# Two half-experts move from plain products to block products, and pure weight blocks are fetched raw, split and written back

## The chip, the cores and the metric

The kernel runs on one core of a Trainium2 chip. The metric is device time in microseconds (us), lower is better; a kernel's time is the median of several runs. Beside the runs there is one profiled execution, whose trace is read here.

## The reference, cut to what matters

```
x   = local_attention(q, k, v)                      # 2304 tokens x 512
x   = elu(x @ w_in) @ w_out                         # first MLP, 2048 hidden
P   = sinkhorn(exp(x @ w_gate - max), 8 rounds)     # 2304 x 8
out = 0
for e in range(8):                                  # w1[e]: 512x1024, w2[e]: 1024x512
    h   = maximum(x @ w1[e], 0)
    out += P[:, e:e+1] * (h @ w2[e])
```

All of it is float32. Only the last loop, the eight experts, is touched by the change.

## The kernel before, in words

TensorE multiplies in the type fp32r. To keep float32 accuracy every operand is split into a high part (a copy rounded to fp32r, made by ACT) and a low part (operand minus high part, made by DVE or POOL), and every product is three matmuls: high·high, high·low, low·high.

The tokens are in three groups of 768 (g = 0, 1, 2), in halves of TH = 384. An expert is two half-experts (512 of its 1024 hidden columns each; index 2·e + pp). A half-expert can be done for a group in two ways.

*Plain*: ordinary products (`e_in` for the first layer, `e_out` for the second). The first PU half-experts are done so, for group 0 alone.

*Block products*: the operands are cut 2x2, and seven products of sums of blocks (`l1` first layer, `l2` second layer) stand for eight. One half-expert of one group is a **period** of seven steps. A step has two `l1` products (6 matmuls of 384 columns each) and one `l2` product; `l2` runs LAG = 8 steps behind `l1`. Of the seven weight blocks of such a set three are **pure**, that is, plain blocks of w1 or w2 (slots 0 to 2), and four are sums (slots 3 to 6). Periods run over the rest of group 0, then all half-experts of group 1, then of group 2.

Split weight blocks lie in DRAM (`wd1`, `wd2`: slot, high and low part) before a period reads them. They are made in three places: `q_tasks(.., "pre")` in the middle of the first MLP (N1 half-matrices), `p_tasks` from the last quarter of the first MLP through the plain stage (N3 half-matrices first, then for each plain unit its four and some others in between, paced by the table `due`), and `late_tasks` in the first block-product periods (`tail`). In `p_tasks` POOL makes the sums, ACT and DVE split them, and SP issues the loads and stores; a half-matrix whose split form a plain unit needs keeps it in SBUF too.

In the block-product stage the order on each engine's queue is the order in which the program emits. `w1_load` and `w2_load` (SP) fetch blocks NW1 = 12 and NW2 = 7 products ahead. After a product ACT copies its PSUM tile out (`a`, `u`, `v`, `r`), DVE adds (`c`, `s`), ACT makes high parts (`h`), DVE or POOL low parts (`hid_low`). PSUM holds two tiles `la`, two `lb`, and one each of `oa` and `ob`. A chain accumulates its `la` tile over several products, so the next product into it waits for the copy; the products 7 and 4 of a chain share one `lb` tile, so product 4 waits for DVE to have read product 7 (the add into `c22`), and the product 7 of the next chain needs the tile that the add into `c21` frees. In group 0 DVE also adds each `l2` product into `acc`.

## Time and profile before

| | |
|---|---|
| median of 3 runs | 1964.22 us (1964.12 to 1965.58) |
| time of the profiled execution | 1965.19 us |
| its span, first to last instruction | 1963.4 us |
| TensorE busy in the span | 1948.9 us |
| granted TensorE clock, mean | 0.999 of full speed |
| plain stage in the trace | from about 499 to 809 us |
| block products of group 0 in the trace | from 809.27 us, seven periods |

The profiled execution is 0.97 us above the median of the runs, so a difference worked out in its trace is set against the median. Where the profile groups matmuls, their durations overlap; the distance from start to start is the cost of one.

### The profile page before, as it was taken

How to read it: one execution, taken by the hardware profiler on the slowest of the kernel's cores; microseconds unless marked ns; L12 is line 12 of the kernel's file. 1: busy time of each engine (PE TensorE's matmuls, PEld its weight loads, DVE VectorE, ACT ScalarE, POOL GpSimd, SP SyncE). 2: the span in 40 equal slices, each digit the busy share in tenths (PEclk: the TensorE clock that was granted, in tenths of full speed). 3: DMA queues.
4: the chain of work that ended last, by engine and by line, in shares of the span. 5: the costliest groups of instructions: out<-in, count | busy, mean ns of one | idle time of the engine just before them, and what ended most of it. 6: DMA issues, size and time to landing. Idle time of an engine off the chain costs nothing.

```text
span 1963.4 us, 33821 instructions
## 1 busy us (share of the span) xinstructions
PE 1948.9 (99%) x11898; PEld 1818.1 (93%) x11898; DVE 1509.2 (77%) x2567; ACT 860.4 (44%) x1821; POOL 732.0 (37%) x718
## 2 busy tenths in 40 slices
PE   8999999999999999999999999999999999999999
PEld 6888888898888888999999999999999999999998
DVE  6756676767797655687787888888887888888886
ACT  8885555555543433444343333333334333333332
POOL 4523232334355553443343333233253333232231
PEclk9999999999999999999999999999999999999999
DMA  9742354469799999699778777788888887777783
GB/s 205 191 93 56 107 173 151 153 219 323 274 377 378 378 361 340 235 360 340 242 249 310 259 260 263 240 275 259 293 263 253 256 271 263 261 261 260 235 280 118
DMA packets 311191, 495.17 MB, mean 252 GB/s; under 512 B 80352, under 2 KB 162416, under 8 KB 307312
## 3 DMA queue, kind: packets, MB, share of 16 engines
q1 hardware_dynamic: 309840, 492.73, 76.2%
q8 instruction: 95, 1.56, 0.3%
q14 instruction: 72, 0.59, 0.1%
q10 hardware_dynamic: 1184, 0.30, 0.1%
HBM read 361.78 MB, written 126.95 MB: 249 GB/s over the span
## 4 chain that ended last, share of the span: by engine, by line
PE 95%; ACT 3%; DVE 2%; DMA 0%; issue 0%; SPq 0%; DVEq 0%; ACTq 0%
PE la L1127 16%; PE lb L1127 12%; PE oa L1207 12%; PE ob L1207 11%; PE ob L1272 3%; PE oa L1272 3%; PE p L932 3%; PE p L933 3%; PE p L934 3%; PE ac L950 3%; PE ac L951 3%; PE p L213 3%; PE p L212 3%; PE ac L547 3%; PE ac L548 3%; PE ac L549 3%
## 5 line engine op out<-in xcount | busy, mean ns | idle before, releaser
L1109 POOL TENSOR_TENSOR h<-s,h 128x384 fp32r<-128x384 f32 x312 | 363.7, 1181 | 725.6 <-ACT h L1100 700.3
L1127 PE MATMUL la<-xf,w1f 128*128 128x384 f32 x1872 | 369.6, 335 | 1.4 <-ACT u L1147 1.3
L1127 PEld LDWEIGHTS la<-xf,w1f 128*128 128x128 f32 x1872 | 326.4, 188 | 2.6 <-ACT u L1147 2.1
L1127 PE MATMUL lb<-xf,w1f 128*128 128x384 f32 x1404 | 281.1, 334 | 0.0
L1100 ACT ACTIVATE h<-s 128x384 fp32r<-128x384 f32 x312 | 159.2, 522 | 246.8 <-DVE s L1151 239.8
L1207 PE MATMUL ob<-h,w2f 128*128 128x384 f32 x1344 | 252.3, 335 | 0.0
L1207 PE MATMUL oa<-h,w2f 128*128 128x384 f32 x1344 | 252.0, 335 | 0.2 <-DVE acc L1224 0.2
L1127 PEld LDWEIGHTS lb<-xf,w1f 128*128 128x128 f32 x1404 | 246.1, 188 | 0.0
L1207 PEld LDWEIGHTS oa<-h,w2f 128*128 128x128 f32 x1344 | 234.4, 188 | 0.5 <-DVE acc L1224 0.5
L1207 PEld LDWEIGHTS ob<-h,w2f 128*128 128x128 f32 x1344 | 234.4, 188 | 0.1
L1105 DVE SCALAR_TENSOR_TENSOR h<-c,h 128x384 fp32r<-128x384 f32 x234 | 193.0, 835 | 32.2 <-ACT h L1100 31.4
L1100 ACT ACTIVATE h<-c 128x384 fp32r<-128x384 f32 x234 | 122.8, 525 | 176.0 <-DVE c L1137 161.8
L739 POOL TENSOR_TENSOR sw<-rw 128x256 f32<-128x256 f32 x104 | 94.8, 912 | 183.8 <-DVE g L775 110.9
L1137 DVE TENSOR_TENSOR c<-c,pb 128x384 f32<-128x384 f32 x192 | 144.5, 752 | 6.6
L1224 DVE TENSOR_TENSOR acc<-ob,acc 128x768 f32<-128x768 f32 (+1 forms) x114 | 105.0, 924 | 37.4 <-PE ob L1207 37.4
L1224 DVE TENSOR_TENSOR acc<-oa,acc 128x768 f32<-128x768 f32 (+1 forms) x110 | 101.2, 923 | 37.3 <-PE oa L1207 37.3
L1151 DVE SCALAR_TENSOR_TENSOR s<-c,s 128x384 f32<-128x384 f32 x156 | 109.7, 703 | 13.4 <-DMA out_dram<-ost 2.4
L1147 ACT ACTIVATE v<-la 128x384 f32<-128x384 f32 x78 | 38.3, 491 | 162.0 <-PE la L1127 161.9
L254 ACT ACTIVATE hh<-p 128x512 fp32r<-128x512 f32 (+1 forms) x72 | 35.3, 490 | 161.9 <-PE p L934 161.7
L932 PE MATMUL p<-xh,f 128*128 128x256 f32 (+1 forms) x288 | 97.8, 339 | 0.0
L933 PE MATMUL p<-xl,f 128*128 128x256 f32 (+1 forms) x288 | 96.9, 336 | 0.0
L934 PE MATMUL p<-xh,f 128*128 128x256 f32 (+1 forms) x288 | 96.9, 336 | 0.0
(176 smaller groups left out, 3895.4 us busy)
## 6 DMA issues: line engine op xcount, KB each, us to landing
w1f<-wdi SPq DMA_DIRECT2D x546, 256.0 KB, 3.9
w2f<-wdo SPq DMA_DIRECT2D x273, 512.0 KB, 4.1
rw<-in_moe_w_dram SPq DMA_DIRECT2D x208, 128.0 KB, 4.8
wdi<-g SPq DMA_DIRECT2D x26, 1024.0 KB, 7.0
wdo<-g SPq DMA_DIRECT2D x26, 1024.0 KB, 7.4
wdi<-f SPq DMA_DIRECT2D x26, 768.0 KB, 5.1
wdo<-f SPq DMA_DIRECT2D x26, 768.0 KB, 5.3
raw<-in_moe_w_in_dram SPq DMA_DIRECT2D x16, 512.0 KB, 4.2
```

The source lines that it names most:

```text
L932: nc.tensor.matmul(p1[:, :n], w[:, s, 0, cs], xh, start=(c == 0), stop=False)
L933: nc.tensor.matmul(p1[:, :n], w[:, s, 0, cs], xl, start=False, stop=False)
L934: nc.tensor.matmul(p1[:, :n], w[:, s, 1, cs], xh, start=False, stop=(c == NCC - 1))
L1100: nc.scalar.activation(h[:, 0], src, AF.Relu if relu else AF.Copy)
L1105: nc.vector.scalar_tensor_tensor(h[:, 1], src, 0.0, r(h[:, 0]), op0=ALU.max, op1=ALU.subtract)
L1109: nc.gpsimd.tensor_tensor(out=h[:, 1], in0=src, in1=r(h[:, 0]), op=ALU.subtract)
L1127: nc.tensor.matmul(o, w[:, a, c, :], x[:, b, c, :], start=first and c == 0 and z == 0, stop=last and c == 1 and z == 2, skip_group_check=True,
L1137: nc.vector.tensor_tensor(out=t, in0=t, in1=pb[g, e][:, i], op=ALU.mult)
L1151: nc.vector.scalar_tensor_tensor(d[nm], d[a], 0.0, d[b], op0=ALU.max, op1=op)
L1207: nc.tensor.matmul(o[:, c], w[:, p, b, c * P:(c + 1) * P], hs[p][:, a, :], start=fresh and p == 0 and z == 0, stop=False, skip_group_check ...
L1224: nc.vector.tensor_tensor(out=a, in0=src, in1=a, op=ALU.add)
L1272: nc.tensor.matmul(o[:, c * HB2:(c + 1) * HB2], hs[p][:, a, c * P:(c + 1) * P], w[:, p, b, :], start=fresh and c != 1 and p == 0 and z == ...
```

## The change: what it does

- PU goes from 9 to 7: two half-experts of group 0 move from the plain stage to block products, which has 41 periods where it had 39. N1, N3 and the tail become 11, 10 and 5 half-matrices; the ten others are spread evenly over the plain units (`mids`), one or two for each, and `p_tasks` splits no pure blocks for half-matrices that no plain unit uses.
- Pure blocks are no longer stored by `p_tasks` or `q_tasks`; these store the sums alone.
- In the nine group-0 periods, and in the first seven periods of group 1, pure blocks are loaded raw from w1 or w2 (`raw_at`) into tiles `r1` (4 buffers) and `r2` (3), half the bytes of a split block. `w_part` makes the high part on ACT and the low part on POOL (w1), or on DVE in group 0 and POOL in group 1 (w2). `w_back` stores the split block to DRAM, where later groups read it. Such a period has six raw w1 blocks and three raw w2 blocks.
- To make room NW1 goes from 12 to 9 and NW2 from 7 to 6. `w_part` stands four `l1` products, or two steps, ahead of its use, in the emitted order.

```diff
-    PU, N1, N3 = 9, 9, 9
-    tail = [(E - 1) * 2 * NP + i for i in (5, 6, 7)]
+    PU, N1, N3, LATE = 7, 11, 10, 5
+    tail = list(range(E * 2 * NP - LATE, E * 2 * NP))
...
-        if u >= 2 and rest:
-            hs.insert(1, (rest.pop(0), u % 4))
+        for i, h in enumerate(mids[u]):
+            hs.insert(2 * i + 1, (h, None))
...
-            p_high(h, 0)
+            if h not in quiet:
+                p_high(h, 0)
...
-    NW1, NW2, LAG = 12, 7, 8
+    NW1, NW2, LAG = 9, 6, 8
...
+    def raw_at(k, s):
+        g, e, pp = periods[k]
+        return s < 3 and (g == 0 or (g == 1 and 2 * e + pp < PU))
+
+    def w_part(key):
+        if key not in apart:
+            return
+        a, hi, lo, t, to, g = apart.pop(key)
+        nc.scalar.activation(hi, a, AF.Copy)
+        sub = nc.gpsimd if key[0] == 1 else (nc.vector, nc.gpsimd)[g]
+        sub.tensor_tensor(out=lo, in0=a, in1=r(hi), op=ALU.subtract)
+        back[key] = (to, t)
+
+    def w_back(key):
+        if key in back:
+            to, t = back.pop(key)
+            nc.sync.dma_start(out=to, in_=t)
...
+        for n in range(4):
+            w_part((1, n))
+        w_back((1, 0))
...
                     w1_load(s * 2 + z + NW1)
+                    w_part((1, s * 2 + z + 4))
+                    w_back((1, s * 2 + z + 1))
...
+            ahead = 0 if s == 3 else s - LAG + 2
+            if s == 3 or ahead > 0:
+                w_part((2, ahead))
+            w_back((2, 0 if s == 4 else s - LAG + 1))
             while late:
                 late.pop(0)()
```

How this moves instructions shows at three places. The first is DVE's queue in the first block-product period, after its step 3. Names: `s` and `c` are the sums, `lb` the PSUM tile, `w2f` a split w2 block, `r_8338` a raw one. Before:

```order
L1151 SCALAR_TENSOR_TENSOR s_9002<-c_8938,r_9000 128x384 [waits DMAHW0_49,Activation_49]
L1151 SCALAR_TENSOR_TENSOR s_9004<-c_8974,r_9000 128x384
L1151 SCALAR_TENSOR_TENSOR s_9006<-c_8938,s_9004 128x384 [waits DVE_49]
L1141 TENSOR_TENSOR c_9024<-lb,u 128x384 [waits PE_49]
L1151 SCALAR_TENSOR_TENSOR s_9026<-c_9024,s_9006 128x384 [waits DVE_49]
L1141 TENSOR_TENSOR c_9037<-lb,a 128x384 [waits PE_49]
```

And of the change, at the same place:

```order
L1185 SCALAR_TENSOR_TENSOR s_8348<-c_8276,r_8346 128x384 [waits Activation_49]
L1185 SCALAR_TENSOR_TENSOR s_8350<-c_8314,r_8346 128x384
L1185 SCALAR_TENSOR_TENSOR s_8352<-c_8276,s_8350 128x384 [waits DVE_49]
L1064 TENSOR_TENSOR w2f<-r_8338,w2f 128x2x256 [waits DMAHW3_49,Activation_49]
L1175 TENSOR_TENSOR c_8375<-lb,u 128x384 [waits PE_49]
L1185 SCALAR_TENSOR_TENSOR s_8377<-c_8375,s_8352 128x384 [waits DVE_49]
L1175 TENSOR_TENSOR c_8388<-lb,a 128x384 [waits PE_49]
```

The low part of the first raw w2 block now stands ahead of the add `c<-lb,u`, and waits for ACT's high part, which stands behind the high part of `s_8352` on ACT's queue.

The second place is DVE's queue in the first period of group 1, steps 4 and 5, where group 0's last `l2` products are still added into `acc`. Before:

```order
L1288 SCALAR_TENSOR_TENSOR acc_103<-oa,Pr,acc_103 128x256 [waits PE_49]
L1288 SCALAR_TENSOR_TENSOR acc_103<-oa,Pr,acc_103 128x256 x2
L1167 TENSOR_TENSOR c_11725<-lb,v 128x384 [waits Activation_49]
L1137 TENSOR_TENSOR c_11725<-c_11725,pb 128x384 [waits DVE_49]
L1288 SCALAR_TENSOR_TENSOR acc_103<-ob,Pr,acc_103 128x256 [waits PE_49]
L1288 SCALAR_TENSOR_TENSOR acc_103<-ob,Pr,acc_103 128x256 x2
```

Of the change:

```order
L1322 SCALAR_TENSOR_TENSOR acc_103<-oa,Pr,acc_103 128x256 [waits PE_49]
L1322 SCALAR_TENSOR_TENSOR acc_103<-oa,Pr,acc_103 128x256 x2
L1064 TENSOR_TENSOR w2f<-r_11884,w2f 128x2x256 [waits DMAHW5_49,DMAHW4_49,Activation_49]
L1201 TENSOR_TENSOR c_12142<-lb,v 128x384 [waits Activation_49]
L1171 TENSOR_TENSOR c_12142<-c_12142,pb 128x384 [waits DVE_49]
L1322 SCALAR_TENSOR_TENSOR acc_103<-ob,Pr,acc_103 128x256 [waits PE_49]
L1322 SCALAR_TENSOR_TENSOR acc_103<-ob,Pr,acc_103 128x256 x2
L1064 TENSOR_TENSOR w2f<-r_11936,w2f 128x2x256 [waits DMAHW6_49,DMAHW0_49,Activation_49]
```

A low part of a w2 block follows the adds into `acc` in steps 4, 5 and 6 of a group-0 period.

The third place is SP's queue late in group 0. DMAHW0 to DMAHW7 are eight semaphores taken in turn: each transfer waits for the one eight before it. Before, in one step and a half:

```order
L1079 DMA w2f<-wdo_0_159 128x1024 [waits DMAHW7_49,PE_49]
L1068 DMA w1f<-wdi_2_141 128x512 [waits DMAHW0_49,PE_49]
L828 DMA wdo_1_162<-qf 128x2x512 [waits DMAHW1_49,DVE_49,Activation_49]
L1068 DMA w1f<-wdi_2_141 128x512 [waits DMAHW2_49,PE_49]
L1079 DMA w2f<-wdo_0_159 128x1024 [waits DMAHW3_49,PE_49]
L1068 DMA w1f<-wdi_3_142 128x512 [waits DMAHW4_49,PE_49]
```

Of the change (`r_` raw blocks, `wdi<-w1f` and `wdo<-w2f` the stores):

```order
L1107 DMA r_9927<-in_moe_w_dram 128x2x256 [waits DMAHW7_49]
L1086 DMA r_9944<-in_moe_w_dram 128x2x128 [waits DMAHW0_49,Pool_49]
L1070 DMA wdi_2_137<-w1f 128x512 [waits DMAHW1_49]
L1092 DMA w1f<-wdi_0_139 128x512 [waits DMAHW2_49,PE_49]
L1070 DMA wdi_3_138<-w1f 128x512 [waits DMAHW3_49,Pool_49]
L1113 DMA w2f<-wdo_1_158 128x1024 [waits DMAHW4_49]
L1092 DMA w1f<-wdi_0_139 128x512 [waits DMAHW5_49,PE_49]
L1092 DMA w1f<-wdi_0_139 128x512 [waits DMAHW6_49]
L1113 DMA w2f<-wdo_1_158 128x1024 [waits DMAHW7_49]
L1086 DMA r_10057<-in_moe_w_dram 128x2x128 [waits DMAHW0_49]
```

A period that had 21 transfers of 7.34 MB has 30 of 8.91 MB (14 w1 blocks, six of them raw with six stores; seven w2 blocks, three of them raw with three stores).

## Rows read from the trace of the kernel before

**Rows 1.** The page: busy time of the engines, share, instructions

```profile
PE 1948.9 (99%) x11898; PEld 1818.1 (93%) x11898; DVE 1509.2 (77%) x2567; ACT 860.4 (44%) x1821; POOL 732.0 (37%) x718
```

**Rows 2.** Waits of PE: who for whom, us in total, times, longest

```profile
PE la L1127 <- ACT u L1147: 1.3, 2, 1.0
```

**Rows 3.** PE's timeline, plain stage (start, us): a unit's start, four units later

```profile
641.35 0.39 PE L932 MATMUL p<-xh,f 128*128 128x512 f32 x1
...
773.51 0.39 PE L932 MATMUL p<-xh,f 128*128 128x512 f32 x1
```

**Rows 4.** PE's timeline, step 2 of periods: group 0 five apart; group 1 two apart

```profile
861.30 2.25 PE L1127 MATMUL la<-xf,w1f 128*128 128x384 f32 x12
...
1009.47 2.25 PE L1127 MATMUL la<-xf,w1f 128*128 128x384 f32 x12
...
1039.03 2.24 PE L1127 MATMUL la<-xf,w1f 128*128 128x384 f32 x12
...
1097.27 2.24 PE L1127 MATMUL la<-xf,w1f 128*128 128x384 f32 x12
```

**Rows 5.** Stretches: us, PE, PEld, DVE, ACT, POOL busy, clock, DMA share, GB/s

```profile
600.00:650.00 50.00, 50.00 (x257) 42.73 (x256) 34.52 (x44) 21.55 (x31) 29.37 (x35) 1.00 1.05 382
850.00:900.00 50.00, 50.00 (x357) 50.00 (x357) 40.98 (x76) 21.95 (x47) 22.27 (x22) 1.00 1.01 371
...
956.27:985.67 29.40, 29.40 (x211) 29.40 (x210) 22.13 (x44) 10.93 (x23) 11.03 (x9) 1.00 0.75 240
985.67:1015.07 29.40, 29.40 (x210) 29.40 (x209) 25.49 (x46) 14.73 (x28) 17.44 (x13) 1.00 0.81 273
```

**Rows 6.** Groups by form, 840 to 1000 us: busy, mean ns

```profile
L823 DVE TENSOR_TENSOR qf<-qw,qf 128x512 fp32r<-128x512 f32 x8 | 7.9, 992 | 0.0
...
L843 POOL TENSOR_TENSOR qw<-qw 128x256 f32<-128x256 f32 x12 | 9.5, 793 | 3.7 <-DVE qf L823 1.8 <-ACT a L1147 1.3
```

**Rows 7.** POOL's timeline at the start of the block products

```profile
803.14 3.64 POOL L1025 TENSOR_TENSOR xf<-xb,xf 128x768 fp32r<-128x768 f32 x2
818.50 5.17 POOL L1109 TENSOR_TENSOR h<-s,h 128x384 fp32r<-128x384 f32 x4 [11.72 <-ACT h L1100]
```

**Rows 8.** ACT's timeline there

```profile
818.96 0.94 ACT L1100 ACTIVATE h<-s 128x384 fp32r<-128x384 f32 x2 [0.54 <-DVE s L1151]
```

**Rows 9.** DVE's timeline there

```profile
813.56 0.56 DVE L1105 SCALAR_TENSOR_TENSOR h<-c,h 128x384 fp32r<-128x384 f32 x1 [1.35 <-ACT h L1100]
...
818.37 0.56 DVE L1151 SCALAR_TENSOR_TENSOR s<-c,s 128x384 f32<-128x384 f32 x1
818.84 0.55 DVE L1141 TENSOR_TENSOR c<-lb,u 128x384 f32<-128x384 f32 x1
...
820.61 2.19 DVE L1105 SCALAR_TENSOR_TENSOR h<-c,h 128x384 fp32r<-128x384 f32 x2
```

**Rows 10.** PE's timeline there

```profile
809.27 1.23 PE L1127 MATMUL la<-xf,w1f 128*128 128x384 f32 x6
...
819.70 1.21 PE L1127 MATMUL lb<-xf,w1f 128*128 128x384 f32 x6
...
822.86 1.81 PE L1272 MATMUL ob<-w2f,h 128*128 128x256 f32 x13 [0.19 <-DVE h L1105]
```

**Rows 11.** DVE's timeline, start of group 1

```profile
1012.34 0.55 DVE L1167 TENSOR_TENSOR c<-lb,v 128x384 f32<-128x384 f32 x1
...
1025.75 0.54 DVE L1167 TENSOR_TENSOR c<-lb,v 128x384 f32<-128x384 f32 x1
```

**Rows 12.** PE's timeline, the products that these adds let start

```profile
1014.75 1.20 PE L1127 MATMUL lb<-xf,w1f 128*128 128x384 f32 x6
...
1027.45 1.20 PE L1127 MATMUL lb<-xf,w1f 128*128 128x384 f32 x6
```

**Rows 13.** DMA issues, 820 to 1000 us: KB each, median us to landing

```profile
w1f<-wdi SPq DMA_DIRECT2D x89, 256.0 KB, 4.8
...
qw<-in_moe_w_dram SPq DMA_DIRECT2D x12, 128.0 KB, 5.8
```

More of the change, by code (lines that the diff above doesn't have):

```diff
@@ L701 @@
     rest = others[N1 + N3:]
+    mids = [[]]
+    for u in range(1, PU):
+        mids.append(rest[len(rest) * (u - 1) // (PU - 1):len(rest) * u // (PU - 1)])
     for u in range(PU):
         hs = [(4 * u + i, 4 + (4 * u + i - 4) % 8 if u else i) for i in range(4)]
-        if u >= 2 and rest:
-            hs.insert(1, (rest.pop(0), u % 4))
+        for i, h in enumerate(mids[u]):
+            hs.insert(2 * i + 1, (h, None))
         order += hs
@@ L760, in p_high @@
     def p_high(h, part):
-        n = 3 if part == 0 and h in quiet else 4
         b = slot_of[h]
@@ L768, in p_high @@
         src = (sws if part else rws)[h]
-        nc.scalar.activation(t[:, :n, 0, :], src[:, :n], AF.Copy)
+        nc.scalar.activation(t[:, :, 0, :], src, AF.Copy)
     def p_low(h, part):
-        n = 3 if part == 0 and h in quiet else 4
         t = (sums if part else forms)[h]
@@ L826, in low @@
             )
-            if a >= 4:
-                nc.sync.dma_start(out=to[:, a - 1:a + 1], in_=r(t))
-            else:
-                for i in range(n):
-                    s = [s for s in pos if pos[s] == a + i][0]
-                    nc.sync.dma_start(out=to[:, s], in_=r(t[:, i]))
+            nc.sync.dma_start(out=to[:, a - 1:a + 1], in_=r(t))
         def sums():
@@ L849, in q_tasks @@
             return load, [
[L850 to L852 removed]
+                sums, *[nothing] * 2, lambda: high(4, 2), lambda: (low(4, 2), high(6, 2)),
+                lambda: low(6, 2), *[nothing] * 2,
             ]
         return [
[L855 to L856 removed]
+            load, nothing, sums, nothing, lambda: high(4, 2),
             lambda: (low(4, 2), high(6, 2)), lambda: low(6, 2),
@@ L889, in highs @@
         def highs():
-            p_high(h, 0)
+            if h not in quiet:
+                p_high(h, 0)
             if n:
-                p_store(before, 1)
+                p_store(before)
         def last():
-            p_low(h, 0)
+            if h not in quiet:
+                p_low(h, 0)
             p_load(n + 3)
@@ L1067, in w1_load @@
         t = P2["w1p"].tile([P, 2, 2, P], R32, tag="w1", bufs=NW1, name="w1f")
-        nc.sync.dma_start(
-            out=r(t).rearrange("p z c f -> p z (c f)"), in_=wd1[e][2 * pp + p][:, SLA[pi]]
-        )
+        s = SLA[pi]
+        to = wd1[e][2 * pp + p][:, s]
+        if raw_at(k, s):
+            f, d = [fd for fd, v in PURE[0].items() if v == s][0]
+            f0 = f * (FF // 2) + (2 * pp + p) * P
+            a = P2["w1p"].tile([P, 2, P], F32, tag="r1", bufs=4, name="r1")
+            nc.sync.dma_start(
+                out=a,
+                in_=w1[e][d * 2 * P:(d + 1) * 2 * P, f0:f0 + P].rearrange("(c p) f -> p c f", p=P),
+            )
+            apart[1, n] = (a, t[:, 0], t[:, 1], r(t).rearrange("p z c f -> p z (c f)"), to, g)
+        else:
+            nc.sync.dma_start(out=r(t).rearrange("p z c f -> p z (c f)"), in_=to)
         w1t[n] = t
@@ L1078, in w2_load @@
         t = P2["w2p"].tile([P, 2, 2, HB2], R32, tag="w2", bufs=NW2, name="w2f")
-        nc.sync.dma_start(out=r(t), in_=wd2[e][pp][:, SLB[out_order[x]]])
+        s = SLB[out_order[x]]
+        to = wd2[e][pp][:, s]
+        if raw_at(k, s):
+            f, d = [fd for fd, v in PURE[1].items() if v == s][0]
+            f0 = f * (FF // 2) + 2 * pp * P
+            a = P2["w2p"].tile([P, 2, HB2], F32, tag="r2", bufs=3, name="r2")
+            nc.sync.dma_start(
+                out=a,
+                in_=w2[e][f0:f0 + 2 * P, d * HB2:(d + 1) * HB2].rearrange("(q p) d -> p q d", p=P),
+            )
+            apart[2, n] = (a, t[:, :, 0], t[:, :, 1], r(t), to, g)
+        else:
+            nc.sync.dma_start(out=r(t), in_=to)
         w2t[n] = t
```

28 lines of the change are left out of this document (10 added, 18 removed).

## The prediction

> **What bounds the kernel now.** I read the page first: PE is busy 1948.9 us of a span of 1963.4 [rows 1]. The rest is 14.5 us, about half of it in the first 50 us. The table of waits comes next: in all of the block products the largest wait of PE is 1.3 us in two pieces, for the copy `u` [rows 2]. The stretches then show PE at 50.00 of 50 us even where the DMA engines are saturated, at 382 GB/s in the plain stage and 371 in the first block products [rows 5]. So the kernel is bound by the matmuls that PE is given. DMA, POOL and ACT cost nothing as long as they are not late. The reader should take from this that a change can win only by giving PE fewer columns, and loses whatever new waits of PE it makes. DVE deserves a look too: 25.49 of 29.40 us in the period before group 1 [rows 5], with less slack than anything but PE.
>
> **What the change takes from PE.** A plain unit (one half-expert for group 0) starts at 641.35, the fifth at 773.51, so one lasts (773.51 - 641.35) / 4 = 33.04 us [rows 3]. A group-0 period lasts (1009.47 - 861.30) / 5 = 29.63 us [rows 4]. Two half-experts change from one to the other: 2 x (33.04 - 29.63) = 6.82 us less. Periods of groups 1 and 2, 29.12 us each [rows 4], keep their matmuls and their number. No PE wait elsewhere is there to be removed, so 6.8 us is the most that the change can bring.
>
> **What it adds, where hidden.** In a raw period ACT makes nine more copies. Two of 384 columns take 0.94 us [rows 8], so one of 256 or 512 is bounded by 0.4 and 0.7 us, together at most 4.5 us on top of 14.73 of 29.40 [rows 5]: hidden. POOL makes six subtractions of 256 columns at 0.79 us [rows 6], 4.8 us on top of 17.44 in its fullest period [rows 5]. In group 1 it makes three of 512 as well, 0.8 to 1.9 us each (the row of 256 and half of the 3.64 us that two of 768 take [rows 7]); I take 1.6, so 9.6 us on POOL in a raw period of 29.12 us. All this is hidden on average.
>
> At the stage's start POOL's last form ends at 803.14 + 3.64 = 806.78 [rows 7]; two low parts at 0.79 follow and the first is ready at 807.6, the second at 808.4, before PE's first product at 809.27 [rows 10]. If that 0.9 us of cover went, PE would wait by as much. In the plain stage 34 half-matrices are prepared in six units where 39 were in eight: POOL's work in a unit grows by about a sixth of 29.37 of 50 us [rows 5], DVE's and ACT's stays, the stores of pure blocks fall away. I cost it at nothing, at most 1 us if a form came late for its unit.
>
> **DVE, first place: the start of the block products.** In the first period the low part of the first raw w2 block stands ahead of the add `c<-lb,u`. In the trace the last `s` ends at 818.37 + 0.56 = 818.93, and that add stood at 818.84, with no gap [rows 9]. ACT's two high parts for `s` run from 818.96 [rows 8]; the new copy falls between them, at about 819.4, and ends about 820.0. The subtraction of 128x512 takes 0.99 us by the nearest row, for the same form [rows 6], so it ends near 821.0. The add then ends near 821.5. The product into the tile that it frees started at 819.70 [rows 10]: 1.85 us of wait. The chain behind (another `s`, the next `c`, two `h`) moves on by about 2.2 us, and the first `l2` product, which waited for it till 822.86 [rows 10], moves with it. I take 2.1 us; the bounds are 1.5 (a subtraction of 0.6 us, and POOL idle) and 2.8 (the raw block landing late: a load takes 4.8 to 5.8 us [rows 13], and is issued about 5 us after the stage starts).
>
> **DVE, second place: the start of group 1.** From about 997 to 1038 us DVE works almost without a gap: group 1's forms and scalings beside group 0's adds. Three low parts of w2 blocks come into this stretch, 3 x 0.99, and POOL's extra work slows DVE somewhat (below). The add `c<-lb,v` at 1012.34 ended 1.86 us ahead of the product that needs it, the one at 1025.75 only 1.16 us [rows 11, 12]. By then DVE would be about 2.3 and 2.4 us later (two low parts, 0.7 us of contention; after a gap, another low part): waits of 0.4 and 0.8 us, so 1.2 us. Bounds: 0, if gaps absorb it, and 2.5, if nothing does. In the other group-0 periods the same adds have 1.3 to 2 us to spare and DVE has gaps of some 4 to 7 us (22.13 of 29.40 busy [rows 5]); I take nothing.
>
> **DMA.** A raw period moves 8.91 MB where it moved 7.34: 8.91 / 29.63 us = 301 GB/s, under the 371 and 382 that the trace shows [rows 5]. In the first periods the tail's five half-matrices and the filling of w2 come on top. From the queue's order the periods' loads and stores sum to 7.9, 12.6, 11.5 and 10.5 MB, so 42.5 MB in four periods, 358 GB/s; the two worst need 425 and 389. At 371 GB/s (11.0 MB a period) the queue falls behind by 1.6 + 0.5 MB, some 6 us. A raw w1 block is issued five products, some 10.5 us, before ACT reaches its copy, and lands in about 5.8 us [rows 13]; the queue usually runs some products ahead of that, but the late stores make it wait for DVE. If 6 us of lag met 4.7 us of margin, ACT would hold up PE's copies by 1.3 us, of which a step covers most. I take 0.9 us, between 0 and 4.
>
> The sum: -6.82 + 2.1 + 1.2 + 0.9 = -2.6 us. The profiled execution, 1965.19 us, would become 1962.6. It stood 0.97 us above the median, and against that median of 1964.22 the forecast is **1961.6 us**, 0.13% less. Differences within 0.2%, 3.9 us, I count as no change; about that much can be told from none here.
>
> **A rule weighed against the rows.** DVE's low part `h<-c,h` takes 0.56 us alone at 813.56, and 2.19 us for two at 820.61, while POOL is busy from 818.50 to 823.67 [rows 7, 9]: an operation on two SBUF tiles is slowed, at most twofold. Work of POOL costs DVE about 0.2 us for each us here if their operations meet a third of the time, so 4.8 us of new POOL work costs some 1 us in a group-0 period, as taken above. The Trainium skill, "SBUF — State Buffer", section "SBUF: two separate sides", has it harder: VectorE with two SBUF inputs and GpSimd hold a shared port pair in turn, for the whole instruction, and the loser is blocked. Each 0.79 us subtraction could then stop DVE for its length. The trace agrees in kind (twofold at worst); in how often they meet it decides, and the full blocking is the third rival.
>
> **The rivals.**
>
> *Faster: the waits are hidden.* The new adds meet gaps; only part of the first place is left. With waits of 1.5 to 2.9 us the time is 1964.22 - 6.82 + 1.5 to 2.9, about 1959.2; with none it is 1957.4. For it: six periods in the trace go by with no wait at all and DVE at 75% to 87%. Against: the first place has its order written down, and no gap ahead of `c<-lb,u` [rows 9]. Chance 0.33.
>
> *Slower: the DMA queue cannot keep up.* Sixteen periods run raw. If blocks in pieces of 512 bytes and stores among loads lower the rate, raw blocks come after ACT has reached their copies, the copies `u` and `v` queue behind, and PE waits in every period. At 290 GB/s a period would take 8.91 / 0.290 = 30.7 us: 9 x 1.1 + 7 x 1.6 = 21 us, less some 9 us of lead (nine products are some 19 us; after landing split blocks keep 13 of them, raw ones 5), so +12, and with the other terms (-6.8 + 3.3) +8.6, 1972.8. At 300 it would decide near +3. For it: 358 GB/s are wanted over four periods. Against: the plain stage ran at 382 with raw loads and stores mixed [rows 5]. Chance 0.12.
>
> *No change, by another way: POOL blocks DVE.* If each new POOL subtraction stopped DVE for its whole length, a usual group-0 period had 22.13 + 3.0 + 4.8 = 29.9 of 29.63 us and the one before group 1 25.49 + 7.8 = 33.3: waits of about 8 x 0.3 + 3.7 = 6.1 us beside the first place's 2.1, so 1964.22 - 6.82 + 8.2 = 1965.6. Against: POOL's and DVE's operations meet only in part, since most adds read PSUM. Chance 0.10.
>
> My forecast itself has 0.45. So faster by over 0.2% 0.33, within 0.2% 0.55, slower 0.12. For the range: below 1957.4 nothing is left; the faster cases begin there, 1957.8 leaves out very little, and 1966.5 takes in the blocked DVE and a mild DMA lag. About 0.15 lies outside. The likeliest case's own range, from its bounds (1.5 to 2.8, 0 to 2.5, 0 to 4, cut at the bound for faster), is 1960.3 to 1964.5.
>
> **What would show it.** Right: two plain units fewer at 33.0 us, and two periods more at 29.6; a wait of PE of about 2 us for DVE's `c` or `h` within 15 us of the first block product; DVE above 95% in the period before group 1 with waits under 1 us each; landing of raw blocks below 8 us. Wrong: PE waiting for ACT's `u` and `v`, with ACT waiting for DMA, in many periods (the queue), or steady small waits for `c` in each raw period (the ports), or a start of group 1 as free of waits as before (the waits are hidden).

## The result, and the profile after

The changed kernel takes 1981.91 us (median of 4 runs, 1980.77 to 1983.18), the kernel before 1964.9 beside it: a ratio of 1.0086, 95% interval 1.0069 to 1.0104. The forecast of 1961.6 and its range up to 1966.5 were wrong; the change is slower by 17 us. The profiled execution has a span of 1981.4 us, 18.0 more than before.

The first line, of the page of the changed kernel, is to be read beside [rows 1]: PE still is nearly always busy. The view behind it cuts the trace at the starts of units and periods (columns: stretch, its length, busy time and instructions of PE, PEld, DVE, ACT and POOL, granted clock, share of the DMA engines, GB/s):

```profile
PE 1946.5 (98%) x11982; PEld 1820.6 (92%) x11982; DVE 1546.0 (78%) x2604; ACT 898.3 (45%) x1949; POOL 875.8 (44%) x851
```

```profile
538.92:577.24 38.32, 35.86 (x181) 29.09 (x180) 33.83 (x60) 17.73 (x23) 28.88 (x30) 1.00 0.93 310
577.24:614.31 37.07, 35.02 (x181) 29.18 (x180) 33.93 (x65) 14.04 (x20) 22.69 (x25) 1.00 0.79 262
...
749.20:769.70 20.50, 18.54 (x103) 18.22 (x102) 11.09 (x20) 10.34 (x24) 9.35 (x10) 0.92 0.94 318
796.50:828.50 32.00, 30.46 (x213) 29.74 (x212) 28.72 (x49) 15.96 (x36) 17.16 (x18) 1.00 1.03 372
858.80:890.00 31.20, 29.86 (x212) 29.54 (x211) 26.26 (x48) 14.27 (x33) 15.81 (x15) 1.00 1.03 371
979.00:1008.60 29.60, 29.60 (x212) 29.60 (x212) 24.44 (x46) 15.85 (x34) 20.43 (x18) 1.00 0.91 295
1008.60:1042.50 33.90, 30.54 (x212) 29.63 (x211) 32.79 (x53) 14.88 (x32) 18.59 (x16) 1.00 0.69 238
1042.50:1078.00 35.50, 31.05 (x176) 30.73 (x175) 25.58 (x40) 15.91 (x34) 19.08 (x18) 0.95 0.94 326
```

The reader is to see that the loss is not spread: the period at 979 takes the usual 29.6 us [rows 4], while two plain units (38.32 and 37.07 us, before 35.00 and 34.59), the first periods and the two periods at the start of group 1 are long. From here on the stages are measured as distances between the first product of one unit or period and that of the next, in each kernel's trace. "No new wait" is the kernel before, with two plain units of 33.04 us less and two periods of 29.63 us more; it is not the forecast, which added 4.2 us of waits. In the table the early periods are the first five of the block products; a time is the median of a kernel's runs, two to eleven of them (before, beside them, 1963.9 to 1964.9), and the stages are from one trace of each.

| kernel | time, us | plain stage | early periods | first of group 1 | second |
|---|---|---|---|---|---|
| no new wait | 1957.4 | 243.86 | 132.45 | 29.63 | 29.20 |
| **after** | 1981.9 | 249.65 | 140.85 | 33.96 | 35.50 |
| e1_mids | 1976.4 | 243.91 | 140.77 | 33.99 | 34.37 |
| e2_w2pool | 1983.1 | 249.77 | 140.66 | 33.37 | 36.97 |
| e3_halves | 1981.5 | 249.68 | 140.97 | 33.99 | 34.60 |
| e5_spread | 1979.4 | 249.75 | 138.01 | 33.99 | 34.87 |
| e6_shared | 1984.7 | 249.73 | 142.54 | 33.98 | 35.38 |
| e7_w2zero | 1979.0 | 249.66 | 137.00 | 31.81 | 36.64 |
| e8_w1zero | 1980.7 | 249.71 | 142.04 | 31.79 | 34.59 |
| f1_lead | 1985.2 | 249.75 | 143.24 | 33.15 | 32.93 |
| f2_out | 1980.7 | 249.74 | 141.44 | 33.99 | 34.53 |
| f3_first | 1983.4 | 249.75 | 141.85 | 33.99 | 35.96 |
| f4_all | 1972.4 | 243.82 | 134.73 | 33.55 | 34.49 |
| g1_sum | 1967.5 | 243.87 | 135.99 | 33.30 | 32.21 |
| g2_order | 1969.6 | 243.82 | 136.41 | 34.89 | 31.17 |
| g3_zeros | 1976.3 | 249.65 | 137.18 | 30.94 | 35.01 |
| g4_twice | 2022.7 | 249.67 | 163.49 | 31.88 | 38.13 |
| **h1_last** | 1966.0 | 243.83 | 134.14 | 33.30 | 29.20 |
| h2_stored | 1973.4 | 243.83 | 140.69 | 30.65 | 29.20 |

So the 18 us are -6.8 (the forecast for PE) + 5.8 in the plain stage + 8.4 in the early periods + 4.3 and 6.3 about group 1's start. The early periods of after, e3, e6 and f2, whose program is the same up to there, range from 140.8 to 142.5, the third of them alone from 31.4 to 35.0: smaller differences are not read. PE's waits in the whole trace of the changed kernel (columns: who waited for whom, us, times, longest) name a different releaser for each place; [rows 2] are those of the kernel before.

```profile
PE la L1161 <- ACT v L1181: 4.9, 2, 4.5
...
PE csum L640 <- DVE cs L636: 4.5, 4, 1.3
PE lb L1161 <- DVE c L1175: 3.6, 3, 2.0
PE lb L1161 <- DVE c L1201: 3.1, 3, 1.2
PE la L1161 <- ACT u L1181: 1.6, 2, 1.1
```

The timeline of the changed kernel at four of these waits (columns: start, length, engine, line, operation, tiles, number, and in brackets the idle time ahead and its releaser):

```profile
547.79 1.72 POOL L742 TENSOR_TENSOR sw<-rw,sw 128x256 f32<-128x256 f32 x1
549.54 1.06 ACT L771 ACTIVATE g<-sw 128x1024 fp32r<-128x1024 f32 x1 [2.86 <-POOL sw L742]
550.50 0.58 ACT L254 ACTIVATE hh<-p 128x512 fp32r<-128x512 f32 x1
551.12 0.69 DVE L255 SCALAR_TENSOR_TENSOR hl<-p,hh 128x512 fp32r<-128x512 f32 x1 [2.21 <-ACT hh L254]
554.74 0.42 DVE L636 TENSOR_REDUCE cs<-Pr 128x8 f32<-128x144 f32 x1
555.21 0.39 PE L640 MATMUL csum<-cs,ones 128*128 128x8 f32 x2 [1.10 <-DVE cs L636]
...
761.74 1.39 PE L1161 MATMUL lb<-xf,w1f 128*128 128x384 f32 x6 [1.96 <-DVE c L1175]
762.93 2.12 PE L1161 MATMUL la<-xf,w1f 128*128 128x384 f32 x6
...
1005.74 2.29 POOL L1064 TENSOR_TENSOR w1f<-r,w1f 128x256 fp32r<-128x256 f32 x2
1007.36 3.22 DVE L1185 SCALAR_TENSOR_TENSOR s<-c,r 128x384 f32<-128x384 f32 x2
1008.00 2.15 POOL L1017 TENSOR_TENSOR xf<-xb,xf 128x768 fp32r<-128x768 f32 x1
...
1052.22 0.39 SPq L1325 DMA_DIRECT2D out_dram<-acc  x1
1058.47 0.81 ACT L1256 ACTIVATE acc<-oa 128x768 f32<-128x768 f32 x1 [6.49 <-DMA r<-in_moe_w_dram]
1059.18 0.48 ACT L1181 ACTIVATE v<-la 128x384 f32<-128x384 f32 x1
1059.72 2.24 PE L1161 MATMUL la<-xf,w1f 128*128 128x384 f32 x6 [4.45 <-ACT v L1181]
```

Four chains stand there. POOL's sums (`sw`) hold ACT's `g`, behind it stands `hh`, DVE waits for that, and the Sinkhorn step `csum` comes late. ACT's waits for these sums from 530 to 610 us, in the changed kernel and then before:

```profile
ACT g L771 <- POOL sw L742: 22.9, 10, 5.3
```

```profile
ACT g L769 <- POOL sw L739: 8.2, 3, 4.0
```

The second is the wait that the prediction calls the first place. The third is two adds `s` of DVE that take 3.22 us beside POOL. Last, ACT's first copy into group 1's accumulator waits, and `v` behind it; the wait is put down to a raw block, but the last output store, issued at 1052.22 and landing after 6.1 us, ends at 1058.3 as well. In the kernel before the same copy waited for the same store, and PE did not (ACT's timeline there, then PE's):

```profile
1041.55 0.82 ACT L1222 ACTIVATE acc<-oa 128x768 f32<-128x768 f32 x1 [3.90 <-DMA out_dram<-acc]
1042.26 0.48 ACT L1147 ACTIVATE v<-la 128x384 f32<-128x384 f32 x1
...
1043.19 1.20 PE L1127 MATMUL la<-xf,w1f 128*128 128x384 f32 x6
```

There `v` ended 0.45 us ahead of the product that needs its tile. The store had been issued 4.9 us ahead of that product and landed after 3.1 us. In the changed kernel it was issued 3.05 us ahead of the time at which the product was due (1055.27, the end of the product before), and landed after 6.1 us. So about 1.85 us of later issue and 3.0 us of longer landing, less 0.45 us of room, make up PE's wait. A half clock followed it (window below, of the changed kernel): the wait and about 1.7 us for 3.4 us at 0.50 are nearly all of the 6.3.

```profile
1060.00:1063.00 3.00, 3.00 (x10) 3.00 (x10) 2.34 (x5) 1.57 (x3) 0.73 (x1) 0.50 0.59 120
```

### The profile page after: what moved, and what is told of

Its sections match the earlier page's. It is cut to its first block, busy times and chain, and to the rows that moved or that the text cites. A ratio compares the mean times of both kernels' runs of the same rounds, so it can differ in the third digit from the quotient of the medians.

```text
span 1981.4 us, 34313 instructions
## 1 busy us (share of the span) xinstructions
PE 1946.5 (98%) x11982; PEld 1820.6 (92%) x11982; DVE 1546.0 (78%) x2604; ACT 898.3 (45%) x1949; POOL 875.8 (44%) x851
## 4 chain that ended last, share of the span: by engine, by line
PE 82%; DVE 6%; DMA 6%; ACT 2%; POOL 2%; issue 2%; SPq 1%; POOLq 0%; DVEq 0%; ACTq 0%
PE la L1161 15%; PE oa L1241 11%; PE ob L1241 11%; PE lb L1161 11%; PE ac L547 3%; PE p L212 2%; PE ac L548 2%; PE p L213 2%; PE p L214 2%; PE ac L549 2%; PE oa L1306 2%; PE ob L1306 2%; POOL sw L742 1%; PE p L924 1%; PE p L926 1%
## 5 line engine op out<-in xcount | busy, mean ns | idle before, releaser
L1143 POOL TENSOR_TENSOR h<-s,h 128x384 fp32r<-128x384 f32 x328 | 382.8, 1183 | 618.6 <-ACT h L1134 606.9
L1161 PE MATMUL la<-xf,w1f 128*128 128x384 f32 x1968 | 391.0, 336 | 7.9 <-ACT v L1181 4.9
L1161 PEld LDWEIGHTS la<-xf,w1f 128*128 128x128 f32 x1968 | 344.1, 189 | 10.3 <-ACT v L1181 5.8
L1161 PE MATMUL lb<-xf,w1f 128*128 128x384 f32 x1476 | 297.0, 336 | 6.6 <-DVE c L1175 3.6
L1161 PEld LDWEIGHTS lb<-xf,w1f 128*128 128x128 f32 x1476 | 259.1, 188 | 8.6 <-DVE c L1175 4.4
L1139 DVE SCALAR_TENSOR_TENSOR h<-c,h 128x384 fp32r<-128x384 f32 x246 | 207.7, 854 | 40.7 <-ACT h L1134 39.6
L1064 POOL TENSOR_TENSOR w1f<-r,w1f 128x256 fp32r<-128x256 f32 x96 | 82.2, 866 | 55.7 <-ACT w1f L1062 55.0
L235 DVE SCALAR_TENSOR_TENSOR m<-m,p 128x512 f32<-128x512 f32 (+1 forms) x78 | 50.1, 642 | 59.8 <-ACT m L247 59.6
L1185 DVE SCALAR_TENSOR_TENSOR s<-c,r 128x384 f32<-128x384 f32 x164 | 91.0, 596 | 3.8 <-ACT r L1212 1.5
L547 PE MATMUL ac<-gh,w1h 128*128 128x512 f32 (+1 forms) x240 | 88.7, 370 | 0.0
```

The source lines that it names most:

```text
L547: nc.tensor.matmul(d, wh[:, wc], gh[:, :n], start=f, stop=False)
L1064: sub.tensor_tensor(out=lo, in0=a, in1=r(hi), op=ALU.subtract)
L1139: nc.vector.scalar_tensor_tensor(h[:, 1], src, 0.0, r(h[:, 0]), op0=ALU.max, op1=ALU.subtract)
L1143: nc.gpsimd.tensor_tensor(out=h[:, 1], in0=src, in1=r(h[:, 0]), op=ALU.subtract)
L1161: nc.tensor.matmul(o, w[:, a, c, :], x[:, b, c, :], start=first and c == 0 and z == 0, stop=last and c == 1 and z == 2, skip_group_check=True,
L1185: nc.vector.scalar_tensor_tensor(d[nm], d[a], 0.0, d[b], op0=ALU.max, op1=op)
```

## The experiments

**Theory A**: each long place has its own chain of waits on POOL, ACT and DVE. **Theory B**: the DMA queue cannot bear the raw blocks and write-backs. **Theory C**: GpSimd's (POOL's) new work blocks VectorE (DVE) wherever the two meet.

**e1_mids.**

```diff
-    mids = [[]]
-    for u in range(1, PU):
+    mids = [[], [], []]
+    for u in range(3, PU):
```

> Theory A (the loss sits in three places, each with a waiting chain of its own): the ten half-matrices set between others now come in plain units 3 to 6 only, so that the units in which the Sinkhorn steps run prepare four each. Then POOL's sums no longer hold ACT and, through ACT's copy for hl, DVE: plain units 1 and 2 fall from 38.32 and 37.07 us to about 35.0 and 34.6, the block products change nothing, and the time falls by 5 to 6 us, to about 1976. Theory B (the DMA queue cannot bear the raw blocks): plain units as long as in the changed kernel, 1982. Theory C (GpSimd's added work blocks VectorE wherever it runs): units 3 to 6 become longer by what 1 and 2 lose, about 1981.

The plain stage came back to 243.91 us, 0.05 from the row without a new wait, and the time fell by 5.5. Theory A holds there; units 3 to 6 grew by 0.3 us together, so B and C fail for this place.

**e2_w2pool.**

```diff
-        sub = nc.gpsimd if key[0] == 1 else (nc.vector, nc.gpsimd)[g]
+        sub = nc.gpsimd
```

> The low parts of the raw w2 blocks go from VectorE to GpSimd in group 0 as well. Theory A: VectorE is what is late in the group-0 periods, so the first period falls from 20.51 to about 18 us (the wait of 1.96 us for c goes, and with it perhaps the half clock behind it), the period in which group 1 starts from 33.96 to about 31, and the time by 5 to 8 us, to about 1975. Theory B: the periods 1 to 4 stay at 26.8, 32.0, 30.3 and 31.3 us; no gain over 2 us. Theory C: GpSimd's three subtractions of 128x512 a period, 1.3 us each, cost VectorE as much as they take from it: 1980 to 1986.

The first period came to 17.71 us as A said, but the second and third were 1.6 and 1.4 longer (the third within its range above), and the first of group 1 gained only 0.6. The sum is nothing, as C expected. The work moved, and in the second period the loss moved with it.

**e4_nine.** The raw blocks without the two half-experts.

```diff
-    PU, N1, N3, LATE = 7, 11, 10, 5
+    PU, N1, N3, LATE = 9, 9, 9, 3
```

> Only the raw blocks are left of the change: nine plain half-experts, nine early ones and three late ones as before. Theory A: the plain stage takes about the 309.9 us that it took before; the first period still waits 2 us for c, the two periods about the start of group 1 still lose 8 to 11 us, the periods 1 to 4 lose 1 to 3: 1975 to 1980. Theory B: the same raw traffic with less beside it in the first periods: 1970 to 1975, with the loss in the first five periods gone and none at group 1's start. If all came from the seven plain half-experts, the time would be that of before, 1964.

1983.1 us: plain stage 309.69 us against 309.94 before, early periods 140.05, start of group 1 33.99 and 35.07. So the raw scheme alone costs 19 us, above what A expected; the two half-experts give back only 1.2. Against e1_mids they are worth 1983.1 - 1976.4 = 6.7 us, the term that was forecast; by the stages 309.69 - 243.91 - 2 x 29.63 = 6.5.

**e5_spread.**

```diff
-                    if ltasks and s >= 6:
+                    if ltasks and s >= 6 and (z == 0 or s % 3 == 0):
```

> The steps for the five late half-matrices are taken at two of three products where one was taken at every product, so that they end some 20 products later. If the periods 1 to 4 (26.8, 32.0, 30.3, 31.3 us; 120.3 together, against 115.1 before the change) are long by the crowd of late steps, be it on the DMA queue or on VectorE, they come to about 117, the time falls by 2 to 4 us. If the raw blocks alone make them long, nothing changes by more than 1 us there. The start of group 1 keeps its loss in either case.

The early periods fell by 2.8 us, by 1.2 of it because no half clock followed the first wait (last section). A part of the loss is the crowd of late steps; not all.

**e3_halves and e6_shared.** In e3 group 1 stores its columns in exchanged halves; in e6 it also writes into group 0's tile.

```diff
-            a = acT[:, 2 * j + cs[0]:2 * j + cs[1], ts]
+            a = acT[:, 2 * (1 - j) + cs[0]:2 * (1 - j) + cs[1], ts]
...
-                oa[g] = accp.tile([P, 6, DM], F32, tag="acc2", name="acc2")
+                oa[g] = oa[0]
```

> Groups 1 and 2 keep their accumulator with the two halves of the columns exchanged, so that the first copy into it falls on rows whose output store of group 0 was issued two products earlier. Theory A: ACT no longer waits 6.5 us for the landing of the last output store, the copy v behind it is in time, the wait of 4.45 us of PE at 1059.7 goes, and with it the half clock behind it: the second period of group 1 falls from 35.5 to 29.5 to 31 us, the time by 4 to 6 us. Theory B (ACT waited there for a raw block from the DMA queue, as the wait's name has it): no change, 1982.

> The exchange of halves as before, and besides group 1 writes into group 0's accumulator tile itself and takes no new tile, so that a copy into it waits for the rows that it overwrites and no longer for the last output store. Theory A: ACT's wait of 5.7 to 6.5 us ahead of its first copy into the accumulator goes, v is in time, PE's wait of 3.5 to 4.5 us and the half clock behind it go: the second period of group 1 falls from 35.5 (34.6 with the exchange alone) to 29.2 to 31 us, the time to 1975 to 1978. Theory B, raw blocks late at that place: another wait of PE of 3 us or more takes its place, 1980 to 1982.

In e3 the wait stayed, now under its right name: a new tile waits for the old one as a whole. In e6 it was gone, and about 12 us further on ACT waited 6.7 us ahead of the first of three copies of raw w1 blocks; PE's wait was 2.7 us where it had been 4.45, and the time did not fall (1984.7). That wait has two parts. The raw block was issued at 1060.11, behind the broadcast of the routing weights (11.6 us to land), and landed after 9.0 us, at 1069.1. From then on ACT waited for a write-back store: the copy goes into the buffer of an earlier block, which the store, issued at 1067.38, still read till it landed at 1071.8. The profile names that store. ACT's timeline in e3, and SP's and ACT's in e6:

```profile
1057.35 0.81 ACT L1256 ACTIVATE acc<-oa 128x768 f32<-128x768 f32 x1 [5.69 <-DMA out_dram<-acc]
```

```profile
1060.11 2.60 SPq L1086 DMA_DIRECT2D r<-in_moe_w_dram  x1
...
1067.38 0.39 SPq L1070 DMA_DIRECT2D wdi<-w1f  x1
...
1071.90 0.42 ACT L1062 ACTIVATE w1f<-r 128x256 fp32r<-128x256 f32 x1 [6.70 <-DMA wdi<-w1f]
```

**e7_w2zero, e8_w1zero, g3_zeros.** These leave low parts out. The condition shown is e7's; e8 has `key[0] == 1`, g3 either.

```diff
-        sub = nc.gpsimd if key[0] == 1 else (nc.vector, nc.gpsimd)[g]
-        sub.tensor_tensor(out=lo, in0=a, in1=r(hi), op=ALU.subtract)
+        if key[0] == 2 and g == 0:
+            nc.scalar.activation(lo, a, AF.Copy, scale=0.0)
+        else:
+            nc.gpsimd.tensor_tensor(out=lo, in0=a, in1=r(hi), op=ALU.subtract)
```

> The low parts of the raw w2 blocks of group 0 are not computed: ACT writes zeros there (its room allows 0.6 us each), and VectorE is spared 27 subtractions. It prices VectorE's new work alone. Theory A: the first period falls to about 18 us, the periods 2 to 4 to about 30, the first period of group 1 from 33.96 to 30 to 31; its second period keeps some 35. Together 8 to 10 us, about 1972 to 1974. Theory C (GpSimd's work is what slows VectorE): under 4 us, since 0.7 us of a subtraction alone is little. Theory B: under 3 us.

> The low parts of the raw w1 blocks are not computed: ACT writes zeros there, and GpSimd is spared 96 subtractions of 128x256. It prices GpSimd's new work beside VectorE's. Theory C: VectorE's operations on two SBUF tiles no longer meet them; the first period of group 1 falls from 33.96 to about 31, the periods 2 to 4 to about 30, 6 us or more in all. Theory A: 1 to 4 us, most of it in the first period of group 1. Theory B: under 2 us.

> The changed kernel without the low parts of all raw w1 blocks and of group 0's raw w2 blocks; ACT writes zeros there. Each alone brought the first period of group 1 from 33.96 to 31.8 us. If VectorE's own work and GpSimd's work beside it add up there, it comes to 29.6 to 30 us now; if either is enough for the same gain, it stays at 31 or more. The second period keeps some 34 to 36 us, since no low part is what it waits for.

In the first period of group 1 either took 2.2 us away, both 3.0: VectorE's subtractions and GpSimd's beside them press on the same time. In the early periods only VectorE's counted (-3.9), GpSimd's not at all (+1.2). The times fell by less than theory A said: e7's by 2.9 us where it said 8 to 10, since the second period of group 1 lost 1.1 more, with 6.8 us at a granted clock of 0.50 (3.4 in the changed kernel); e8's by 1.3. The adds `s` that took 3.22 us took 1.02 in e8 at the same place; the kernel before and then e8:

```profile
999.20 1.01 DVE L1151 SCALAR_TENSOR_TENSOR s<-c,r 128x384 f32<-128x384 f32 x2
```

```profile
1009.90 1.02 DVE L1188 SCALAR_TENSOR_TENSOR s<-c,r 128x384 f32<-128x384 f32 x2
```

In these two POOL was idle while they ran; in the changed kernel it had no gap. The Trainium skill, "SBUF — State Buffer", section "SBUF: two separate sides", has VectorE with two SBUF inputs blocked for a whole GpSimd instruction; the trace agrees: 2.2 us more beside a GpSimd instruction of 2.15 us and the end of two that took 2.29 together, three times the usual length, where the prediction held twofold for the most.

**f1_lead, f2_out, f3_first.** The first line pair is f1; f2 is e6 with the middle part (the output stores go into a list, emptied in the step after, behind its `l1` products); the last pair is f3.

```diff
-                    w_part((1, s * 2 + z + 4))
+                    w_part((1, s * 2 + z + 3))
...
+            stores.append(lambda: nc.sync.dma_start(
...
+            while len(stores) > 0:
+                stores.pop(0)()
             if s == LAG - 3:
...
-        sub = nc.gpsimd if key[0] == 1 else (nc.vector, nc.gpsimd)[g]
+        sub = nc.gpsimd if key[0] == 1 or key[1] == 0 else (nc.vector, nc.gpsimd)[g]
```

> ACT and GpSimd take up a raw w1 block three products ahead of its own product where it was four, so that the block has 2.1 us more to land and to be issued; no work is added or dropped. Theory B in its narrow form (SP, held by group 0's output stores and by write-backs, issues raw w1 blocks late, and ACT's queue stands behind them): the second period of group 1 and the periods 2 to 4 lose about 2 us each of their excess, 3 to 6 us in all, 1976 to 1979. Theory A without it: under 1.5 us.

> The shared accumulator with exchanged halves, and group 0's output stores stand one step later in SP's queue, behind the loads of that step, where VectorE has already added the rows. If the wait of 12.4 us of SP for those additions made the raw blocks late, SP waits under 5 us in all there, ACT no longer waits 6.7 us for a raw block, and the second period of group 1 falls from 35.4 to 29.2 to 31 us. If the DMA queue is behind for its bytes, ACT's wait stays, and the period is over 33 us.

> Only the very first low part of a raw w2 block, that of period 0, goes to GpSimd. Theory A: the first period falls from 20.5 (19.33 where no half clock follows the wait) to about 17.7 us, as with all low parts on GpSimd, and the other periods stay as in the changed kernel: 1979 to 1980. If the waits only move on, the second and third period take back 2 us.

f1 took 2.6 us off the second period of group 1, but gave 0.56 us back in each of four later periods, where PE now waits 0.27 us for POOL's low part: 1985.2, slower, where 1976 to 1979 were expected. In f2 SP's longest wait for the adds fell from 12.4 to 7.2 us and the raw block was in time, but the store, later now, landed after 10.8 us and held ACT's next copy by 9.4: the wait moved again. In f3 the first period took 17.65 us, the second took 2.1 of that back, and the third was 2.3 longer, which is within its range above: nothing was won, as the second half of its expectation said.

**f4_all, g1_sum, g2_order.** f4 joins e1, e5, f1, f2, f3 and two more low parts on POOL. g1 goes back to a lead of four and lays the accumulator in eight pieces, so that the first two copies fall on rows stored first. g2 is g1 with DVE's accumulation of a step (`held`) behind the adds of the next.

```diff
+        q = 4 * (i == j) + 2 * j
...
+            a = acT[:, q + cs[0]:q + cs[1]]
...
+        if not 55 <= 7 * k + x <= 61:
+            while held:
+                held.pop(0)()
```

> All of it together: the half-matrices between others in units 3 to 6, late steps at two of three products, raw w1 blocks taken up three products ahead, the shared accumulator with exchanged halves, output stores a step later, and three low parts of raw w2 blocks (the first one and the last two of group 0) on GpSimd. By theory A with the narrow form of B the parts add up: -5.7 in the plain stage, -2.8 in the first period, -2 to -3 in the periods 2 to 4, -5 to -6 in the second period of group 1, -1.2 in the first: 1964 to 1967, as before the change. If the DMA queue is behind for its bytes, 1970 to 1975.

> The sum of the mended places, with raw w1 blocks taken up four products ahead again, as in the changed kernel, and the accumulator's eight pieces laid so that group 1's first two copies fall on rows whose stores were issued first. Theory A with SP's hold: the second period of group 1 falls from 34.5 to about 29.5 us, the 0.56 us in each later raw period of group 1 goes (they came with the lead of three), the first period stays about 18 us, the periods 2 to 4 at 29.6 to 30.2 without the shorter lead; the first period of group 1 keeps its 33.5. About 1964 to 1966. If the DMA queue is behind for its bytes, another wait of 3 us or more stands in the second period: 1969 to 1972.

> The same, and from the last period of group 0 on VectorE makes an accumulation of one step only behind the two adds of the step after, so that what PE waits for goes first; no work is taken away. If VectorE is late there only in the order of its queue, PE's waits of 0.8, 0.3 and 1.2 us in the first period of group 1 shrink and it takes about 31 us: 1961 to 1963. If VectorE has more work than time there, as 33.5 busy of 33.5 us say, the waits move to PE's accumulators (oa, ob for acc) and little is won: 1964 to 1966.

Together the edits of the early periods do what none does alone: 134 to 136 us. f4 took 1972.4 us, above its 1964 to 1967: its second period of group 1 was still 34.49, with a store that landed after 9.7 us, and the lead of three cost its 0.56 us in four periods again. g1's ratio to the kernel before is 1.0017 (1.0008 to 1.0027), 1.5 us above what was expected. What was left in its second period: the last output store, behind the broadcast of the routing weights and two loads, took 10.7 us to land. For the first period of group 1, g2 shows that the order on DVE was not the cause: PE then waits for the accumulations, and the period took 34.89. The rows: g1's store and ACT's timeline, and PE's timeline in g2.

```profile
1052.95 0.81 ACT L1256 ACTIVATE acc<-oa 128x768 f32<-128x768 f32 x1 [5.11 <-DMA out_dram<-acc]
...
DMA to landing us min/median/max: 2.7/7.2/10.7
```

```profile
1012.06 2.21 PE L1305 MATMUL oa<-w2f,h 128*128 128x256 f32 x12 [1.77 <-DVE acc L1321]
```

**g4_twice.** Here `to` is a triple: the place, a second place that nobody reads, and the group.

```diff
-            nc.sync.dma_start(out=to, in_=t)
+            nc.sync.dma_start(out=to[0], in_=t)
+            if to[2] == 0:
+                nc.sync.dma_start(out=to[1], in_=t)
```

> The changed kernel, and each block that is written back in group 0 is written a second time to a place that nobody reads: 3.1 MB more in a period of 8.9. It prices the write-back. Theory B (bytes on the DMA queue): the periods 1 to 4, at 370 GB/s already, grow by 5 us or more together, and the periods 5 to 8, at 12.0 MB or 405 GB/s, grow past 29.63 by 1 us or more each: 10 us or more. Theory A: the periods 5 to 8 stay at 29.63, the periods 1 to 4 grow by under 3 us.

+40.8 us, far beyond what A allowed. By the mean granted clock, 0.991 where the changed kernel has 0.998, some 14 us of it (an estimate: that share of either span) are half clock behind the waits. The stretch below, free of waits in the changed kernel, moves 388 GB/s and holds up PE; ACT's waits ahead of copies of raw blocks come to 66.5 us and are put down to the second stores. The changed kernel, then g4 (windows), then g4's waits from 745 to 1080:

```profile
900.00:950.00 50.00, 50.00 (x357) 50.00 (x356) 38.11 (x75) 23.78 (x54) 23.03 (x23) 1.00 0.94 320
```

```profile
900.00:950.00 50.00, 47.31 (x330) 46.50 (x329) 41.02 (x77) 24.57 (x56) 26.14 (x25) 1.00 1.04 388
```

```profile
ACT w1f L1068 <- DMA wxi<-w1f: 66.5, 24, 7.6
```

So B is right in this: the raw scheme leaves no room for a second write-back. In this program a copy that reuses a buffer waits for both of its stores; whether the bytes or these longer holds cost the time, the run does not separate; and it does not show that the changed kernel's own bytes cost time.

**h1_last, h2_stored.** h1: g1, with the last output store not put off and the broadcast three steps later. h2: h1, with the last expert of group 0 stored split as before the change, and the late steps at every product.

```diff
+            if x == 6:
+                stores.pop()()
...
-            if j == 0 and k + 1 < NPD and periods
+            if j == 3 and k + 1 < NPD and periods
```

> The sum of the mended places, and besides group 0's last output store is no longer put off by a step, and the broadcast loads of the routing weights stand three steps later in SP's queue. In the sum that store was issued behind the broadcast and two loads and took 10.7 us to land, ACT's copy into the accumulator waited 5.1 us for it and PE 2.7 us for the copy u behind that. If that is the whole of what is left there, the store lands within 3 to 6 us, no wait over 0.5 us stands in the second period of group 1, and it takes 29.2 to 29.8 us where it took 32.21: 1964 to 1965. If another wait takes the place once more, 1967.

> As the run beside it, and the last expert of group 0 is left out of the raw scheme: the pure blocks of its eight half-matrices are stored split, three early and five late, as before the change, and its two periods, the last of group 0, load them split. VectorE then has no low part of a raw w2 block near the start of group 1, and ACT and GpSimd none of group 0's raw w1 blocks there; GpSimd keeps those of group 1. The first period of group 1 falls from 33.3 to 30.5 to 31.8 us. The late steps are half as many again and take the periods 1 to 5; if they cost no more than the 3 us that stand there now, 1961 to 1963, below the kernel before; if they bring back the excess of the changed kernel, 1965 to 1967.

In h1 that store lands in at most 7.0 us and the second period of group 1 takes 29.20 us: the chain of the output stores, with the broadcast ahead of the last, was all of its loss (which of h1's two edits did it is not shown). The time is 1966.0 us (1963.0 to 1967.2, 11 runs), a ratio of 1.0006 (0.9997 to 1.0015): no different from the kernel before, and no better. The trace is of the fastest of these, 3.0 us below the median. h2's first period of group 1 took 30.65 us as said, but the early periods went back to 140.69 and the plain stage began at 505.4 us, about 6 later than elsewhere, so 1973.4 in place of at most 1967: the load came back at the places to which it was moved. The rows of h1, its stores and the second period of group 1:

```profile
DMA to landing us min/median/max: 2.6/5.9/7.0
...
1028.30:1057.50 29.20, 29.20 (x176) 29.20 (x175) 26.01 (x38) 15.93 (x34) 20.07 (x19) 1.00 0.94 321
```

## Why the prediction was wrong

- **PE's work, -6.82: right.** 6.7 us between e4_nine and e1_mids. What failed are waits: their terms were 4.2 us in the sum and came to 24.8 us of stage lengths.
- **The plain stage, "I cost it at nothing, at most 1 us": failed, +5.8.** The prediction looked at whether POOL's work fits in a unit, and it does: 28.88 of 38.32 us. The step that failed is the overlap: it did not follow the queue behind ACT's wait for POOL, in the one stretch where PE waits for a chain of small DVE steps. e1_mids shows it.
- **DVE, first place, 2.1 us: right in place and size (1.96), wrong as a price.** In the changed kernel the first period lost 3.2, with a half clock behind the wait. Taking the wait away (f3_first) gained nothing over five periods that the range above lets one read.
- **DVE, second place, 1.2 us (0 to 2.5): mis-sized, 4.3.** The waits stood where forecast (`c<-lb,v` 1.0 and 1.2 us) and one more for `a` (1.1). DVE was busy 32.79 of 33.90 us. The prediction's row for DVE there, 25.49 of 29.40 us, begins 15 us ahead of group 1; in the first period of group 1 itself the kernel before leaves DVE 1.2 us of room (row below). Contention was counted as 0.7 us; two adds alone lost 2.2. It is work and contention together (e7, e8, g3), not the order (g2). The third rival, full blocking, priced 3.7 us here; that it came near is in part luck, for it starts from the same row, and its 0.3 us in each usual group-0 period did not come (29.63 in the sixth to ninth).
- **DMA lag in the early periods, 0.9 us (0 to 4): mis-sized, 5.2 in the second to fifth period.** It was not the lag alone: leaving out VectorE's low parts took 3.9 us of the early periods' 8.4, spreading the late steps 2.8, and f4_all, with e1, e5, f1 and f3, 6.1. The forecast asked only whether a raw block's own bytes are late. The trace has another wait: ACT's copy writes into the buffer of an earlier block and waits till that block's write-back has landed. There are four such waits of 9.8 us in all (rows below). The longest leaves DVE idle for 2.78 us; DVE then works without a gap, and PE waits 0.25, 0.46 and 0.83 us in that period. They are not all of the loss: h1_last has 11.8 us of them, nine of at most 2.6, and early periods of 134.14.
- **A term that was missing, 6.3 us: the second period of group 1.** The step that failed is the path. The prediction stopped at group 0's adds and did not ask who waits for the stores behind them: SP, in whose queue raw loads now stand, and ACT, whose copy waits for the landing and in whose queue `v` stands. The slow rival had "the copies `u` and `v` queue behind", but for want of bytes, in every period; it came at one place, by a late store and its landing. The trace of before had the chain, with 3.90 us of ACT's wait and 0.45 us of room.

The rows: DVE's room in the first period of group 1 before the change; then, in the changed kernel, ACT's waits for write-backs from 740 to 900 us, and ACT's, DVE's and PE's timeline in the third period.

```profile
1001.00:1030.60 29.60, 29.60 (x212) 29.60 (x211) 28.36 (x51) 12.19 (x24) 11.53 (x10) 1.00 0.68 217
```

```profile
ACT w1f L1062 <- DMA wdi<-w1f: 9.8, 4, 3.2
...
809.90 0.42 ACT L1062 ACTIVATE w1f<-r 128x256 fp32r<-128x256 f32 x1 [3.19 <-DMA wdi<-w1f]
811.14 1.10 DVE L1139 SCALAR_TENSOR_TENSOR h<-c,h 128x384 fp32r<-128x384 f32 x1 [2.78 <-ACT h L1134]
825.20 1.31 PE L1161 MATMUL lb<-xf,w1f 128*128 128x384 f32 x6 [0.83 <-DVE c L1201]
```

A sum in the prediction does not come out: the upper bounds of the likeliest case, 2.8, 2.5 and 4, give 1966.7, not 1964.5. The measured time is far beyond either.

Which of the edits joined in f4_all mend the early periods beside e5_spread stays open; alone e1, f1 and f3 did nothing there. f1's lead of three is not needed: h1_last reached 134.14 without it. Why h1's runs spread over 4 us (the kernel before, beside them, over 3.4) is open too.

## What to carry to other kernels

Average busy shares say that work fits, not where it stands: for each instruction added to an in-order queue, follow what stands behind it to the first wait of the engine that sets the time. Raw blocks that pass through another engine before their use can turn a delay of the DMA queue into a delay of that engine's whole queue, and a write-back adds one more: the buffer is free only when the store has landed. Look also for waits that cost nothing yet: a chain with 0.45 us of room is the next to break. A wait taken away in a crowded stretch is only won when the engine behind it has time left.
